# A seventh pair of token blocks, and the operand sums of x moved from the score stage to the expert stage

## The chip, the cores and the metric

The kernel runs on one core of a Trainium2 chip. The metric is device time in microseconds (us), and a shorter time is better. A core has engines that work side by side and wait for each other through semaphores: TensorE (PE in the profile; its weight loads are PEld), VectorE (DVE), ScalarE (ACT), GpSimd (POOL) and SyncE (SP, which here issues nearly all transfers). Each engine works through its own queue in order.

## The reference

The output is x + A(xn) + B(xn), where xn is the layer norm of x (2048 tokens of 512 values, float32).

```python
# A: Fourier mixing, real part
a = einsum("bsd,ed->bse", xn, dft_hid_re);  b = einsum("bsd,ed->bse", xn, dft_hid_im)
A = einsum("ts,bse->bte", dft_seq_re, a) - einsum("ts,bse->bte", dft_seq_im, b)
# B: product-key experts: 32 heads, 64 + 64 keys, 4096 experts, 2 experts per head
q = einsum("nd,dhc->nhc", xn, w_q);  q1, q2 = q[..., :128], q[..., 128:]
s1 = einsum("nhd,ed->nhe", q1, k1);  s2 = einsum("nhd,ed->nhe", q2, k2)
# the 2 best of s1 and of s2 give 4 candidate sums per head; the 2 best of these are the experts
g = softmax(top_s);  ue, ve = u[top_e], v[top_e]
act = gelu(einsum("nd,nhkd->nhk", xn, ue))
B = einsum("nhk,nhk,nhkd->nd", g, act, ve)
```

## The kernel before, in words

The tokens are cut into 16 blocks of 128. Every product of B is made with float16 parts: an operand is split into a high part h and a low part l, and three matmuls (h h, h l, l h) stand for one in float32.

The kernel has three stages. The first, up to about 100 us, makes the layer norm and the Fourier part. The second, the score stage (about 100 to 421 us), makes q and the scores for every block and head group and picks the experts; 128 steps, with a hand-written table `todo` that says which other work is issued at which step: loading and splitting u and v, and sums of operands for the third stage. The third is the expert stage, `part_b` from line 1047 on. It does not gather expert rows. For every block it computes the product with all 4096 rows of u (a "z phase"), applies gelu, multiplies by the gate weights, which are zero for all but the chosen experts, and multiplies the result by all rows of v (a "v phase", `v_part`, 96 matmuls of 128 x 512).

A z phase exists in two forms. A single block (`u_part`, L1095) takes 16 groups of 24 matmuls of 128 x 128: 384. Two blocks together, a pair, can be multiplied with fewer products: for 12 of the 16 groups of u (the three `QUADS`), `z_pair` uses seven products in place of eight for a 2 x 2 block matrix, in Strassen's manner. A product is a `slot` of 24 matmuls (L1168). Some products need a sum of parts of u, which is kept in the DRAM tensor `s_d` and streamed in through a ring of three buffers (`ring_load`), and some need a sum of parts of x, which lies in the tile `x4`. The order of the 21 slots and four plain steps is the string `SEQ`. The slot called 5a, the second of a pair, is the first that reads `x4`. The four remaining groups of u go through `u_part` for both blocks at once (matmuls of 128 x 256). `z_pair` needs VectorE to add products from PSUM (L1204, L1212, L1216) and ScalarE to copy them out and to apply gelu.

The phases before the change are: z(0), z(1), v(0), then for b = 2, 4 .. 12 the pair z(b, b+1), v(b-1), v(b), and at the end z(14), v(13), z(15), v(14), v(15). Thus six pairs and four single blocks.

Between the matmuls of a phase, other work is placed by hand with `put(phase, step, ...)`; a v phase has steps 0 to 7. `G(b, k)` is a one-hot step (`g_mm`): VectorE builds two selection matrices for 16 tokens at a time, L (L1246) and R (L1251, L1254), from the chosen experts, and 32 matmuls (L1256) spread the gate weights over all experts. `W(b, k)` (`w_part`) multiplies them by the gelu values (L1264) and splits the product into two float16 parts (L1271 on ACT, L1272 on VectorE). Four of each are needed for a block before its v phase. The units `U` and `F` are checks: the kernel verifies that the given matrices have the symmetry that its fast Fourier path assumes (`compare`, L1323 on, 68 units `U`) and that the scaled values fit (`fit`, units `F`). They only have to be finished at the end, by `verdict`. `add_x(b)` loads y and x of a block and adds them on POOL (L1314), for all blocks but the last; `finish(b)` (L1318, VectorE) adds the v product, and SP stores it.

The sums of x for a pair are made in the score stage by `sum_x(b, part)` (L817 to L835), at six hand-chosen steps. On POOL: a one-column copy that ties it to its step (L823), one addition of high and low parts, 1024 columns (L824), four subtractions of 256 columns (L829 to L832). Later, on ACT, a rounding to float16 (L794), and on POOL the remainder (L795); then two stores of 256 KB to the DRAM tensor `t_d` (L798). In the expert stage, at the start of v(b), b even, `prep` loads the next two blocks of x into `xb2` (L1077), and SP loads `x4` from `t_d` (L1609). The act tile of a block (`act_tile`) is one of three, used in turn, so that block b+2 takes the one that block b-1 used.

Line by line order on the engines follows the program's order and its data dependencies as the compiler's own scheduler arranges them; some work is moved ahead of its place in the program when its inputs are there.

Of the kernel before, what the change touches and what calls it, by code (L numbers as in the profile page):

```python
# [18 lines left out]
P = 128  # L19
# [10 lines left out]
V1 = 5  # L30
V2 = 9
QUADS = (8, 10, 12, 14), (9, 11, 13, 15), (4, 5, 6, 7)
PAIRS = tuple(range(2, 14, 2))


@with_exitstack
def tile_fnet_peer(ctx, tc, x, ca, cb, c5, wt, wf, wr, wq, kt, ut, vn, out):
# [14 lines left out]
    z_d = dram.tile([NT, P, 3 * P], F16, name="z_d")  # L52
    v_d = dram.tile([16 - V2, P, 4 * D], F16, name="v_d")
    s_d = dram.tile([len(QUADS), 4, P, 4 * D], F16, name="s_d")
    t_d = dram.tile([NT // 2, P, 4 * D], F16, name="t_d")

    stQ = ExitStack()
    PS = [stQ.enter_context(tc.tile_pool(name="psum", bufs=1, space=bass.MemoryType.PSUM))]
# [662 lines left out]
    def part_b(safe, stS, stP, stQ, stE, xt, u_sb, cmp_p, w4):  # L721
# [65 lines left out]
        def scratch(g):  # L787
            return v_sb[g].rearrange("p l c d -> p (l c d)").bitcast(F32)

        def split4(part, t, h, dst, at):  # L790

            l = t.bitcast(F16)[:, 0:2 * D]
            if part == 0:
                nc.scalar.activation(h, t, AF.Copy, scale=behind(one, at))  # L794
                nc.gpsimd.tensor_tensor(l, t, h, op=ALU.subtract)  # L795
                return
            for i, v in enumerate((h, l)):
                nc.sync.dma_start(dst(i), v)  # L798
# [15 lines left out]
            split4(part - 1, s4, v_sb[6].rearrange("p l c d -> p (l c d)")[:, par * 2 * D:par * 2 * D + 2 * D],  # L814
                   lambda i: s_d[qd].rearrange("o p (t l f) -> t l p o f", t=4, l=2)[t, i], at)

        def sum_x(b, part, at=None):  # L817

            n = (0, 2, 4, 4, 7, 5)[PAIRS.index(b)]
            f, t4 = scratch(n), scratch(n + 1)  # L820
            if part == 0:
                v = xq[b // 2]
                nc.gpsimd.tensor_copy(f[:, 0:1], behind(one, at))  # L823
                nc.gpsimd.tensor_tensor(f.rearrange("p (q f) -> p q f", q=2),  # L824
                                        v[:, :, 0].rearrange("p q k n -> p q (k n)"),
                                        v[:, :, 1].rearrange("p q k n -> p q (k n)"), op=ALU.add)
                b11, b21, b12, b22 = [f[:, k * 256:k * 256 + 256] for k in range(4)]
                r = [t4[:, k * 256:k * 256 + 256] for k in range(4)]
                nc.gpsimd.tensor_tensor(r[0], b12, b11, op=ALU.subtract)  # L829
                nc.gpsimd.tensor_tensor(r[1], b22, r[0], op=ALU.subtract)  # L830
                nc.gpsimd.tensor_tensor(r[2], b22, b12, op=ALU.subtract)
                nc.gpsimd.tensor_tensor(r[3], b21, r[1], op=ALU.subtract)  # L832
                return
            split4(part - 1, t4, f.bitcast(F16)[:, 0:2 * D],
                   lambda i: t_d[b // 2, :, i * 2 * D:i * 2 * D + 2 * D], at)  # L835

        SRAW = {}

        def stage_v(g, at, store):
# [159 lines left out]
        if not safe:  # L999
            for n, b in zip((19, 22, 25, 106, 109, 118), PAIRS):  # L1000
                todo[n].append(lambda at, b=b: sum_x(b, 0, at))
                todo[n + (4 if n == 118 else 5)].append(lambda at, b=b: (sum_x(b, 1, at), sum_x(b, 2)))
        for g, n in zip(range(V2, 16), (25, 38, 41, 57, 73, 89, 105)):
            todo[n].append(lambda at, g=g: stage_v(g, at, False))
            todo[n - 3].append(lambda at, g=g: fill_load(1, g))
# [98 lines left out]
        if not safe:  # L1104
            sx = stE.enter_context(tc.tile_pool(name="sx", bufs=1, side="left"))
            x4 = sx.tile([P, 2, 4, 2, P], F16, name="x4")
            PLAIN = [g for g in range(16) if not any(g in q for q in QUADS)]
            SEQ = "1a 5a 2a 6a c 3a 1b 7a 2b 5b 4a 6b c 3b 1c 7b 2c 5c 4b 6c c 3c 7c c 4c".split()

            def turn_q(k, n):  # L1110
                return ("abc" if n % 2 else "cba").index(k)

            OPS = {"1": (0, None, None, 0), "2": (1, None, None, 1), "5": (None, 0, 0, None), "6": (None, 1, 1, None),
                   "3": (None, 3, None, 3), "7": (None, 2, 2, None), "4": (3, None, 3, None)}

        USES = []
        if not safe:
# [393 lines left out]


        phases = [("z", 0), ("z", 1), ("v", 0)]
        for b in range(2, 14, 2):
            phases += [("z", b, b + 1), ("v", b - 1), ("v", b)]
        phases += [("z", 14), ("v", 13), ("z", 15), ("v", 14), ("v", 15)]
        plan = {}

        def put(ph, cg, *fs):
            plan.setdefault((ph, cg), []).extend(fs)  # L1520

        def G(b, k):
            return lambda: g_mm(b, k)
# [16 lines left out]
        for b in range(NT):  # L1540
            ph = ("v", b)
            if b % 2 == 0 and 0 < b < 13:
                nx = phases[phases.index(ph) + 1]
                st = 1 if len(nx) == 2 else 2
                put(ph, 1, G(b + 1, 0))
                put(ph, 3, G(b + 1, 1))
                put(ph, 5, W(b + 1, 0))
                put(ph, 7, W(b + 1, 1), G(b + 1, 2))
                put(nx, st, W(b + 1, 2, True), G(b + 1, 3))
                put(nx, 3 * st, W(b + 1, 3, True))  # L1550
            elif b + 1 < NT:
                for k in range(4):
                    put(ph, 2 * k, W(b + 1, k))
                put(ph, 0, G(b + 1, 2))
                put(ph, 3, G(b + 1, 3))
        for ph in phases[2:]:
            if ph[0] == "z":
                n = 4 * len(ph[1:]) - 2
                put(ph, 5 if len(ph) == 2 else 9, G(ph[1], 0))
                put(ph, 7 if len(ph) == 2 else 12, G(ph[1], 1))  # L1560
        for b in range(14):
            put(("v", b), 3, lambda b=b: compact_d(b + 2))
        if not safe:
            for cg in (1, 3, 5, 7):
                put(("v", 0), cg, F[0])
            for ph, cg in ((("v", 12), 0), (("v", 13), 3), (("v", 14), 3), (("v", 14), 7)):
                put(ph, cg, F[0])
            for ph in phases[3:]:
                if ph[0] == "z":
                    for cg in (8,) if len(ph) == 3 else (1, 3, 4, 5):  # L1570
# [12 lines left out]
            for f, n in ((U, 68), (F[0], NK + 16 - V2), (F[1], 16 + V2)):  # L1583
                assert sum(v.count(f) for v in plan.values()) >= n
        for n, ph in enumerate(phases):
            if ph[0] == "z":
                b = ph[1:]
                for c in b:
                    ACT[c] = BT[c] if c < 2 else act_tile(c)
# [183 lines left out]
```

## Time and profile before

| what | value |
|---|---|
| median of 3 runs | 1130.89 us (1129.87 to 1134.87) |
| the profiled execution | 1132.17 us, span 1130.4 us |
| TensorE clock granted | 0.998 |
| busy: PE, DVE, ACT, POOL | 1114.2, 960.3, 657.5, 319.4 us |
| score stage, 100 to 421 us: busy PE, DVE, POOL | 319.3, 292.2, 258.5 us |
| expert stage, 465 to 1103 us: busy PE, DVE, POOL | 634.3, 532.7, 24.8 us |

The span is the time from the first to the last instruction in the trace; the profiled execution's own time is somewhat longer. Busy time is the time in which an engine had an instruction running; an instruction that is held up after it has begun also counts as busy. A row of a group names the line, the engine, the operation, what is written and read, the number of instructions, then the busy time, the mean of one in ns and the idle time of the engine before them. A row of the timeline names the start, the length and the same, and in brackets how long the engine had been idle before and what ended that.

### The profile page before, as it was taken

What the parts mean: (1) busy time and instruction counts of PE and PEld (TensorE: products, weight loads), DVE (VectorE), ACT (ScalarE), POOL (GpSimd) and SP (SyncE); (2) the same over time, 40 slices, a digit from 0 to 9 for tenths busy, and PEclk for the clock granted to TensorE, in tenths of its full rate; (3) what the DMA queues carried; (4) which work ended last, traced back from release to release, by engine and by line L of the source; (5) the groups of instructions that cost most, each with busy time, mean ns of one, the idle gap of its engine ahead of it and who ended that gap; (6) DMA issues with size and microseconds to landing.
All of it is one profiled execution on the core that took longest, in us unless ns stands there. A gap on an engine that the chain in (4) does not pass through costs nothing.

```text
span 1130.4 us, 28284 instructions
## 1 busy us (share of the span) xinstructions
PE 1114.2 (99%) x11180; PEld 724.4 (64%) x11180; DVE 960.3 (85%) x2873; ACT 657.5 (58%) x1099; POOL 319.4 (28%) x357
## 2 busy tenths in 40 slices
PE   9999999999999999999999999999999999999997
PEld 6455454544545459788588479479569569567763
DVE  7899979989889899976996896896998887889782
ACT  6557598798898465454446446445435535545552
POOL 1416896888889750000000000000010010000000
PEclk9999999999999999999999999999999999999999
DMA  9984455345353315464755755665656756575742
GB/s 274 289 207 171 162 168 197 112 154 190 105 187 103 104 50 190 157 249 143 258 216 184 239 206 199 235 218 187 226 199 215 227 199 225 190 246 167 239 150 106
DMA packets 122540, 213.10 MB, mean 189 GB/s; under 512 B 34580, under 2 KB 62107, under 8 KB 122398
## 3 DMA queue, kind: packets, MB, share of 16 engines
q1 hardware_dynamic: 122096, 211.13, 56.3%
q8 instruction: 89, 1.46, 0.5%
q14 instruction: 53, 0.43, 0.1%
q10 hardware_dynamic: 302, 0.08, 0.1%
HBM read 178.34 MB, written 27.07 MB: 182 GB/s over the span
## 4 chain that ended last, share of the span: by engine, by line
PE 50%; DVE 10%; DMA 3%; ACT 2%; POOL 2%; issue 1%; SPq 0%; DVEq 0%; ACTq 0%; POOLq 0%
PE v L1301 24%; PE z L1168 13%; PE z L1095 10%; PE g L1256 4%; DMA cx<-in_cb_dram 3%; DVE L L1246 2%; DVE vals L956 1%; DVE idx L960 1%; DVE w L1264 1%; DVE act L1272 1%; DVE cx L1351 1%; DVE R L1251 0%; DMA fit<-in_wq_dram 0%; DVE cx L1340 0%; POOL v L824 0%
## 5 line engine op out<-in xcount | busy, mean ns | idle before, releaser
L252 PE MATMUL s<-m,xq 128*128 128x512 f16 x1344 | 297.4, 379 | 1.0 <-ACT ss L952 0.5
L1301 PE MATMUL v<-v,act 128*128 128x512 f16 x1056 | 233.4, 379 | 1.0 <-DMA v<-v_d 1.0
L252 PEld LDWEIGHTS <-xq 128*128 128x128 f16 x1344 | 129.8, 98 | 152.2 <-issue 2.4
L1314 POOL TENSOR_TENSOR y<-y,xr 128x512 f32<-128x512 f32 x15 | 26.1, 1740 | 623.4 <-DMA y<-y_d 383.7
L1246 DVE TENSOR_TENSOR L<-io_lam,cmp 128x2048 f16<-128x2048 f16 x128 | 157.5, 1230 | 26.9 <-PE g L1256 26.8
L1301 PEld LDWEIGHTS <-act 128*128 128x128 f16 x1056 | 101.2, 98 | 118.7 <-issue 1.3
L1095 PE MATMUL z<-xb,u 128*128 128x128 f16 (+1 forms) x2112 | 154.3, 234 | 0.1
L1095 PEld LDWEIGHTS <-u 128*128 128x128 f16 x2112 | 141.4, 98 | 6.6 <-issue 0.2
L956 DVE MAX8 vals<-ss 128x8 f32<-128x64 f32 x896 | 133.5, 216 | 5.6 <-ACT ss L952 5.6
L1301 PE MATMUL v<-v,w 128*128 128x512 f16 x480 | 106.3, 379 | 0.1
L952 ACT ACTIVATE ss<-s,wsc 128x512 f32<-128x512 f32 x120 | 81.4, 682 | 41.2 <-PE s L252 35.1
L1377 ACT ACTIVATE cx<-cx 128x896 f32<-128x896 f32 x64 | 60.4, 944 | 72.6 <-DVE cx L1357 53.2
L1168 PEld LDWEIGHTS <-s 128*128 128x128 f16 x1656 | 94.8, 98 | 0.1
L960 DVE FIND_INDEX8 idx<-vals,ss 128x8 uint16<-128x256 f32 x224 | 93.8, 419 | 0.0
L1271 ACT ACTIVATE act<-w 128x1024 f16<-128x1024 f32 x36 | 48.3, 1357 | 68.3 <-DVE w L1264 68.0
L1301 PEld LDWEIGHTS <-w 128*128 128x128 f16 x480 | 45.9, 98 | 53.6 <-issue 0.4
L1168 PE MATMUL z<-x,s 128*128 128x128 f16 x1248 | 78.1, 219 | 0.0
L1168 PEld LDWEIGHTS <-u 128*128 128x128 f16 x1296 | 74.9, 98 | 1.8 <-issue 1.4
L1256 PEld LDWEIGHTS <-L 128*128 128x128 f16 x2048 | 60.3, 96 | 12.7 <-issue 2.1
L1351 DVE TENSOR_TENSOR cx<-cx 128x512 f32<-128x512 f32 (+2 forms) x84 | 48.4, 613 | 23.5 <-DMA cx<-in_cb_dram 23.5
L1264 DVE SCALAR_TENSOR_TENSOR w<-act,scl,g 128x1024 f32<-128x1024 f32 x44 | 55.8, 1277 | 10.3 <-ACT act L1195 10.3
L1256 PE MATMUL g<-R,L 128*128 128x32 f16 x2048 | 61.9, 176 | 1.6 <-DVE R L1254 1.5
(363 smaller groups left out, 1802.3 us busy)
## 6 DMA issues: line engine op xcount, KB each, us to landing
v<-v_d SPq DMA_DIRECT2D x67, 512.0 KB, 4.3
s<-s_d SPq DMA_DIRECT2D x59, 512.0 KB, 4.8
cx<-in_cb_dram SPq DMA_DIRECT2D x64, 448.0 KB, 4.7
w<-in_wq_dram SPq DMA_DIRECT2D x28, 512.0 KB, 6.0
fit<-in_wq_dram SPq DMA_DIRECT2D x28, 512.0 KB, 4.3
uv<-in_vn_dram SPq DMA_DIRECT2D x16, 512.0 KB, 3.5
uv<-in_ut_dram SPq DMA_DIRECT2D x16, 512.0 KB, 4.2
s_d<-v SPq DMA_DIRECT2D x24, 256.0 KB, 3.7
```

Source lines behind the costliest of these rows:

```text
L252: nc.tensor.matmul(ps, xt[i][:, l, kd, :], m[:, r, kd, :], start=(n == 0), stop=(n == 3 * KD - 1))
L952: nc.scalar.activation(s, ps, AF.Copy, scale=inv)
L956: nc.vector.max(vals[:, i, w, :, h], s[:, g, :])
L960: nc.vector.max_index(idx[:, i, w].rearrange("p k h -> p (k h)"), vals[:, i, w, 0:2].rearrange("p k h -> p (k h)"), s[:, w * HC:g + 1, :]. ...
L1095: nc.tensor.matmul(ps if n == 1 else ps.rearrange("p (b n) -> p b n", b=2), ug[:, l, c % 2, kd, :], xb2[:, k0, r, kd, :] if n == 1 else xb ...
L1168: nc.tensor.matmul(bank[:, t * P:(t + 1) * P], lt, rt, start=(t == k == 0 and op in "125"), stop=(t == 3 and k == 5), skip_group_check=op ...
L1246: nc.vector.tensor_tensor(L.rearrange("p t (l two) -> p t l two", two=2), io_lam.rearrange("p (l two) -> p l two", two=2).unsqueeze(1).to_ ...
L1256: nc.tensor.matmul(p[:, hf, t * NC:(t + 1) * NC], L[:, t, :], R[:, t, :], start=True, stop=True)
L1264: nc.vector.scalar_tensor_tensor(w, act[:, :, ts], fw, p.rearrange("p h (n c) -> p c (h n)", c=NC), op0=ALU.mult, op1=ALU.mult)
L1301: nc.tensor.matmul(pv, w16[:, c, :, l], v_sb[g][:, r, cc, :], start=(n + cc == 0 and k == 0), stop=(n == 15 and cc == 1 and k == 2))
L1351: nc.vector.tensor_tensor(v, v, tv[:, 0:1].to_broadcast([P, len(ix), 256]), op=o)
L1377: later.append(lambda: nc.scalar.activation(tf[:, P:], tf[:, P:], AF.Abs, accum_out=chk[:, n:n + 1]))
```

## The change

The blocks 14 and 15 become a seventh pair: the phases end with z(14, 15), v(13), v(14), v(15). The table `PAIRS` gets the entry 14. `t_d`, `sum_x` and its places in the score stage's table are removed. A new function, `x_sums`, makes the sums of x in the expert stage, at the start of v(b), b even, right after `prep` has issued the loads of the next two blocks: on POOL the addition and four subtractions, from `xb2`, with the not yet used act tile of block b+2 as scratch; at step 5 of the same phase ACT rounds them into `x4`, and POOL writes the remainder into `x4`. The load of `x4` goes. The checks are spread anew: four in each pair phase in place of three, one in v(13) in place of three, three in v(14) as before; the one-hot steps of block 15 go to v(13).

```diff
-PAIRS = tuple(range(2, 14, 2))
+PAIRS = tuple(range(2, NT, 2))
...
-    t_d = dram.tile([NT // 2, P, 4 * D], F16, name="t_d")
...
-        def sum_x(b, part, at=None):
...
-            for n, b in zip((19, 22, 25, 106, 109, 118), PAIRS):
-                todo[n].append(lambda at, b=b: sum_x(b, 0, at))
-                todo[n + (4 if n == 118 else 5)].append(lambda at, b=b: (sum_x(b, 1, at), sum_x(b, 2)))
...
+        def x_sums(b, part):
+
+            s = ACT[b].rearrange("p c n -> p (c n)")
+            f, t4 = s[:, 0:2 * D], s[:, 2 * D:4 * D]
+            if part == 0:
+                nc.gpsimd.tensor_tensor(f.rearrange("p (q f) -> p q f", q=2),
+                                        xb2[:, :, 0].rearrange("p q k n -> p q (k n)"),
+                                        xb2[:, :, 1].rearrange("p q k n -> p q (k n)"), op=ALU.add)
+                b11, b21, b12, b22 = [f[:, k * 256:k * 256 + 256] for k in range(4)]
+                r = [t4[:, k * 256:k * 256 + 256] for k in range(4)]
+                nc.gpsimd.tensor_tensor(r[0], b12, b11, op=ALU.subtract)
+                nc.gpsimd.tensor_tensor(r[1], b22, r[0], op=ALU.subtract)
+                nc.gpsimd.tensor_tensor(r[2], b22, b12, op=ALU.subtract)
+                nc.gpsimd.tensor_tensor(r[3], b21, r[1], op=ALU.subtract)
+                return
+            h, l = [x4[:, n].rearrange("p o k n -> p (o k n)") for n in range(2)]
+            nc.scalar.activation(h, t4, AF.Copy)
+            nc.gpsimd.tensor_tensor(l, t4, h, op=ALU.subtract)
...
-        for b in range(2, 14, 2):
+        for b in range(2, NT, 2):
             phases += [("z", b, b + 1), ("v", b - 1), ("v", b)]
-        phases += [("z", 14), ("v", 13), ("z", 15), ("v", 14), ("v", 15)]
+        phases += [("v", 15)]
...
+        put(("v", 13), 5, G(15, 0))
+        put(("v", 13), 7, G(15, 1))
...
-        for b in range(14):
+        for b in range(13):
             put(("v", b), 3, lambda b=b: compact_d(b + 2))
+        put(("z", 14, 15), 8, lambda: compact_d(15))
...
-                    for cg in (9, 12, 15) if len(ph) == 3 else (0, 2, 3, 6):
+                    for cg in (9, 11, 13, 15):
                         put(ph, cg, U)
                 elif ph[1] < 14:
                     for cg, f in enumerate((None, F[1], F[1], None, U, U, U, F[0]) if ph[1] % 2 == 0 else (
-                            None, F[1], None, None, U, U, U, F[0])):
-                        if f:
+                            None, F[1], F[0], None, U, U, U, F[0])):
+                        if f and (ph[1] < 13 or f != U or cg == 6):
                             put(ph, cg, f)
...
-                if phases[n + 1][1] in PAIRS and not safe:
-                    nc.sync.dma_start(x4.rearrange("p l o k n -> p (l o k n)"), t_d[phases[n + 1][1] // 2])
+                c = phases[n + 1][1]
+                if c in PAIRS and not safe:
+                    ACT[c] = act_tile(c)
+                    x_sums(c, 0)
+                    put(ph, 5, lambda c=c: x_sums(c, 1))
```

More of the change, by code (lines that the diff above doesn't have):

```diff
@@ L815, in sum_u @@
                    lambda i: s_d[qd].rearrange("o p (t l f) -> t l p o f", t=4, l=2)[t, i], at)
-        def sum_x(b, part, at=None):
[L819 to L835, printed above, removed]
         SRAW = {}
@@ L998, in part_b @@
                 todo[n + 5].append(lambda at, g=g: (sum_u(g, 1, at), sum_u(g, 2)))
-        if not safe:
-            for n, b in zip((19, 22, 25, 106, 109, 118), PAIRS):
-                todo[n].append(lambda at, b=b: sum_x(b, 0, at))
-                todo[n + (4 if n == 118 else 5)].append(lambda at, b=b: (sum_x(b, 1, at), sum_x(b, 2)))
         for g, n in zip(range(V2, 16), (25, 38, 41, 57, 73, 89, 105)):
@@ L1555, in part_b @@
                 put(ph, 3, G(b + 1, 3))
+        put(("v", 13), 5, G(15, 0))
+        put(("v", 13), 7, G(15, 1))
         for ph in phases[2:]:
             if ph[0] == "z":
-                n = 4 * len(ph[1:]) - 2
-                put(ph, 5 if len(ph) == 2 else 9, G(ph[1], 0))
-                put(ph, 7 if len(ph) == 2 else 12, G(ph[1], 1))
-        for b in range(14):
+                put(ph, 9, G(ph[1], 0))
+                put(ph, 12, G(ph[1], 1))
+        for b in range(13):
             put(("v", b), 3, lambda b=b: compact_d(b + 2))
+        put(("z", 14, 15), 8, lambda: compact_d(15))
         if not safe:
@@ L1565, in part_b @@
                 put(("v", 0), cg, F[0])
-            for ph, cg in ((("v", 12), 0), (("v", 13), 3), (("v", 14), 3), (("v", 14), 7)):
+            for ph, cg in ((("v", 12), 0), (("v", 14), 1), (("v", 14), 3), (("v", 14), 7)):
                 put(ph, cg, F[0])
@@ L1569, in part_b @@
                 if ph[0] == "z":
-                    for cg in (8,) if len(ph) == 3 else (1, 3, 4, 5):
+                    for cg in (8,):
                         put(ph, cg, F[0])
-                    for cg in (9, 12, 15) if len(ph) == 3 else (0, 2, 3, 6):
+                    for cg in (9, 11, 13, 15):
                         put(ph, cg, U)
@@ L1588, in part_b @@
                 for c in b:
-                    ACT[c] = BT[c] if c < 2 else act_tile(c)
+                    if c not in ACT:
+                        ACT[c] = BT[c] if c < 2 else act_tile(c)
                 def after(cg):
```

## The prediction

> **What bounds the kernel now.** First the page's head, to see which engine is full; then the waits of TensorE in the expert stage alone, from 421 us to the end, because a busy share over the whole span says nothing of one stage. (A wait's columns: us in total, times, longest.)
>
> ```profile
> span 1130.4 us, 28284 instructions
> PE 1114.2 (99%) x11180; PEld 724.4 (64%) x11180; DVE 960.3 (85%) x2873; ACT 657.5 (58%) x1099; POOL 319.4 (28%) x357
> ```
>
> ```profile
> PE g L1256 <- DVE R L1254: 1.5, 3, 1.0
> ...
> PE z L1168 <- ACT act L1215: 0.2, 1, 0.2
> ```
>
> TensorE is busy 99% of the span, and in 710 us of expert stage its five rows of waits make 3.4 us. So matmul time that goes counts in full, and what only relieves another engine counts for nothing, unless TensorE waits for that engine next. How near the others are is read from windows by stage: the scores, v(0), v(6), the last pair z(12,13), and v(13), z(15), v(14). (Columns: window, its length, then busy us of PE, PEld, DVE, ACT, POOL, and the granted clock.)
>
> ```profile
> 100.00:421.00 321.00, 319.33 (x2050) 159.65 (x2048) 292.18 (x1536) 253.74 (x422) 258.53 (x291) 1.00 0.42 136
> 465.00:488.00 23.00, 22.70 (x188) 11.14 (x184) 23.00 (x30) 10.66 (x14) 0.00 (x0) 1.00 0.66 231
> 725.00:748.00 23.00, 23.00 (x187) 11.56 (x185) 18.70 (x30) 7.45 (x12) 1.28 (x1) 1.00 0.59 203
> 923.00:964.00 41.00, 41.00 (x707) 39.93 (x704) 31.74 (x52) 21.84 (x40) 2.36 (x1) 1.00 0.54 191
> 1034.00:1057.00 23.00, 22.70 (x191) 11.31 (x188) 22.97 (x37) 10.04 (x13) 0.00 (x0) 1.00 0.54 192
> 1057.00:1080.00 23.00, 23.00 (x427) 22.65 (x426) 14.62 (x37) 14.47 (x27) 1.28 (x1) 1.00 0.54 172
> 1080.00:1103.00 23.00, 23.00 (x193) 11.65 (x189) 20.27 (x40) 12.29 (x16) 0.00 (x0) 1.00 0.60 184
> ```
>
> VectorE is the second bound, close behind: all of v(0), 18.7 of 23 us in v(6), 31.7 of 41 in a pair. The clock is 1.00 throughout.
>
> **What TensorE saves.** Stretches of the chain of waits (start, length, matmuls) in the last pair, in the single block z(15) and at the end, and the group of the pair's additions:
>
> ```profile
> 928.71 2.62 PE z L1095 x24
> 931.33 0.79 PE g L1256 x32
> 932.12 9.39 PE z L1168 x168
> ...
> 1057.77 16.08 PE z L1095 x288
> ...
> 1099.94 23.97 PE v L1301 x111
> ```
>
> ```profile
> L1204 DVE TENSOR_TENSOR act<-z,act 128x512 f32<-128x512 f32 x9 | 6.2, 686 | 0.0
> ```
>
> A single block takes 384 matmuls at 16.08/288 = 55.8 ns, so z(14) and z(15) cost 768 x 55.8 ns = 42.9 us. As a pair they are 21 slots of 24 matmuls at 9.39/168 = 55.9 ns (28.2 us) and four plain steps of 2.62 us (10.5 us): 38.7 us. The one-hot steps (L1256) and the v phases stay the same in number. Saved: 4.2 us. The pair adds nine VectorE additions of 0.69 us, 6.2 us in a stretch that, by z(12,13), keeps 9 us free: nothing on the path.
>
> **What leaves the scores.** Six times, on POOL, a one-column copy, an addition, four subtractions and a rounding; on ACT two one-column copies and a rounding; on SP two stores; and later, on SP, a load of x4:
>
> ```profile
> L795 POOL TENSOR_TENSOR v<-v,v 128x1024 f16<-128x1024 f32 x18 | 38.4, 2133 | 5.5 <-ACT v L794 5.5
> L824 POOL TENSOR_TENSOR v<-xq 128x1024 f32<-128x1024 f16 x6 | 12.7, 2121 | 0.4
> L831 POOL TENSOR_TENSOR v<-v 128x256 f32<-128x256 f32 x6 | 4.4, 737 | 0.0
> ```
>
> ```profile
> x<-t_d SPq DMA_DIRECT2D x6, 512.0 KB
> s<-s_d SPq DMA_DIRECT2D x59, 512.0 KB, 4.8
> xb<-xt_d SPq DMA_DIRECT2D x14, 256.0 KB, 3.0
> ```
>
> One pair's POOL work is 2.12 + 4 x 0.73 + 2.13 = 7.2 us. In the scores TensorE is busy 319.3 of 321 us, so 43 us less of POOL there are worth 0 to the 1.7 us that TensorE idles. I take 0: it is hidden by TensorE's own work now, and so is its removal. Of DMAs, 6 loads and 12 stores go and about ten loads of s_d come (59 serve six pairs); the DMA engines are at 0.5 to 0.7 in the windows, so 0. On SP the load of x4 stood right behind the loads of xb; what is behind it starts one issue earlier, 0.
>
> **What comes into v(b), b even.** Seven times the same 7.2 us of POOL, in v(0), v(2) to v(12), and a rounding on ACT, which has 12 us and more free there: 0. The first POOL operation waits for xb2's load (3.0 us) and for v(b-1) to free its act tile, so the five start with v(b). Behind them in POOL's queue stands only the addition of y and x for v(b), which VectorE's last step of v(b) needs some 20 us later: 0. x4 is due at the pair's second slot, 24 us after the start, against 7.2 us and ACT's rounding. So POOL is not late. But it does not run beside VectorE for free. Rows of POOL and VectorE around three y additions (start, length):
>
> ```profile
> 560.55 1.22 DVE L1246 TENSOR_TENSOR L<-io_lam,cmp 128x2048 f16<-128x2048 f16 x1
> 560.63 2.26 POOL L1314 TENSOR_TENSOR y<-y,xr 128x512 f32<-128x512 f32 x1 [61.76 <-DVE R L1254]
> 561.71 2.38 DVE L1272 TENSOR_TENSOR act<-w,act 128x1024 f16<-128x1024 f32 x1
> ...
> 996.72 1.39 POOL L1314 TENSOR_TENSOR y<-y,xr 128x512 f32<-128x512 f32 x1 [66.24 <-DVE w L1264]
> 996.89 2.30 DVE L1246 TENSOR_TENSOR L<-io_lam,cmp 128x2048 f16<-128x2048 f16 x1
> 999.12 1.28 DVE L1272 TENSOR_TENSOR act<-w,act 128x1024 f16<-128x1024 f32 x1
> ...
> 1018.30 2.12 POOL L1314 TENSOR_TENSOR y<-y,xr 128x512 f32<-128x512 f32 x1 [20.18 <-DMA y<-y_d]
> 1019.19 1.29 DVE L1264 SCALAR_TENSOR_TENSOR w<-act,scl,g 128x1024 f32<-128x1024 f32 x1
> ```
>
> At 996.9 an L took 2.30 us, not 1.22, because a POOL addition of 1.39 had begun. At 560.6 POOL began while an L ran and took 2.26 us itself, and then VectorE's L1272 took 2.38, not 1.28. They run one after the other, and VectorE loses some 1.1 us to a POOL operation of 1.4. Where VectorE takes an operand from PSUM (the w at 1019.2) it loses nothing.
>
> The Trainium skill (SBUF — State Buffer, "Who interferes with whom") says that a DVE instruction with two SBUF inputs contends with a GpSimd instruction that reads SBUF, and that one with at most one SBUF input, outside the 2-port modes, does not. The trace agrees: 2.30 against 1.22 us, and 1.29 us unharmed. If every VectorE operation stood in the way, the rule would charge 7.2 us at each of seven places, and the sum would be +46 us and not the one below.
>
> What VectorE's loss costs TensorE differs by phase. In v(0), where VectorE never rests (rows of VectorE and TensorE; in brackets the idle time before a row):
>
> ```profile
> 464.59 1.23 DVE L1246 TENSOR_TENSOR L<-io_lam,cmp 128x2048 f16<-128x2048 f16 x1 [1.52 <-PE g L1256]
> 471.44 0.43 DVE L1254 TENSOR_TENSOR R<-R,cmp 128x512 f16<-128x512 f16 x1
> 471.93 0.56 PE L1256 MATMUL g<-R,L 128*128 128x32 f16 x16 [0.19 <-DVE R L1254]
> 489.95 0.43 DVE L1338 TENSOR_TENSOR cx<-cx 128x256 f32<-128x256 f32 x1 [0.56 <-DMA cx<-in_cb_dram]
> ```
>
> VectorE works without a pause from 464.6 to 489.4, and the one-hot matmul at 471.93 starts 0.06 us after its R ends. What VectorE loses ahead of the last one-hot step of v(0), TensorE loses too. The second xb load can only start when z(1) ends at 465, so the sums begin near 468: 2.1 + 4 x 0.73 = 5.0 us in turn with VectorE, and perhaps part of the last 2.1. Bounds 0 (all of it behind the last one-hot step) and 7.2; I take 5.
>
> In the other six there is slack. In v(6), which starts at 725.0:
>
> ```profile
> 730.82 1.23 DVE L1246 TENSOR_TENSOR L<-io_lam,cmp 128x2048 f16<-128x2048 f16 x1 [2.51 <-PE g L1256]
> 745.67 0.46 DVE L1254 TENSOR_TENSOR R<-R,cmp 128x512 f16<-128x512 f16 x1
> 747.37 0.95 PE L1256 MATMUL g<-R,L 128*128 128x32 f16 x32
> ```
>
> VectorE idles 2.5 us before 730.8, and half of the five operations fall there or beside PSUM operations. What is left of them and the rounding of 2.1 us make it some 2.3 us late (between 0 and 5). The one-hot step at 747.37 needs the R that ends at 746.13: 1.2 us of slack. So TensorE waits about 1.1 us. Bounds 0 and 5.0 - 1.2 = 3.8 a phase; I take 1, as v(6) gives, six times: 6.
>
> **The tail.** Until now z(15) lay between v(13) and v(14), and VectorE rested there (14.6 of 23 us). Now v(13) follows the pair and v(14) follows v(13), and the two one-hot steps of z(15), about half of its 14.6 us, go to v(13), from which two checks are taken out. VectorE then has 23.0 + 20.3 + 7.3 less up to 4, some 47 to 50 us, against 2 x 96 matmuls of 23.97/111 us and six steps of 0.79, 46.2 us of TensorE. The checks can go on in v(15), so VectorE need not hold TensorE up; with checks ahead of the last w part it does, by up to 3.8. Bounds -1.5 (the waits for R that there are now go) and 3.8; I take 0.5, near the first, since checks are not waited for.
>
> **Sum.** -4.2 + 5 + 6 + 0.5 = +7.3 us. The profiled execution took 1132.17 us, 1.8 more than its span, and lies 1.3 above the median of 1130.89. On the median: 1130.9 + 7.3 = 1138.2 us.
>
> **Rivals.** (1) TensorE-bound, not slower. POOL's sums land in VectorE's idle time and beside its PSUM operations, and only the 4.2 us show: 1126.7 us; if the old 3.4 us of waits go too, 1123.3. For it: the y additions on POOL cost TensorE no more than 1.5 us in all now. Against it: they are one operation a phase, the sums are six. It decides below 4.2/7 = 0.6 us of wait a pair.
>
> (2) Half of it. v(0) pays and the others absorb, or the reverse: -4.2 + 5 or -4.2 + 6, some 1132 us.
>
> (3) x4 late. ACT's rounding is put at step 5 of 8, some 15 us into v(b), and POOL's last 2.1 to 4 us follow, which leaves about 4 us.
>
> ```profile
> ACT act L1271 <- DVE w L1264: 68.0, 28, 4.6
> ```
>
> A rounding queued behind such a wait, 4.6 us at the longest, makes slot two late by 1 to 2 us: 7 to 14 us on top of -4.2, or of the sum, 1134 to 1152 us.
>
> (4) The last blocks do not run as a pair. The diff leaves no path for it, so it gets no chance of its own.
>
> **How the numbers follow.** 0.5% is 5.7 us, about what a measurement of this kernel can tell from no change. My sum, ending above +5.7: 0.48, its own range 1136.6 to 1149 (with 3 us a phase in place of 1). x4 late or a tail that piles up: 0.07. Half: 0.17. TensorE-bound: 0.28, of which 0.15 stays within 0.5% and 0.13, with old waits gone, passes it. So slower 0.55, same 0.32, faster 0.13. The range must take in most of rival 1: from 1126 to 1149, which leaves out about 0.1 at each end.
>
> **What would show it.** L1168 with 3528 matmuls, not 3024, L1095 with 1440, not 2112, and the last pair in 38.7 us beside its one-hot steps. In v(0), v(2) to v(12), six POOL rows from the phase's start, some far above 0.73 us, and VectorE's L, R and L1272 beside them at twice their time. TensorE's wait for R at 8 to 14 us, not 1.5, some 5 of it in v(0). I am wrong if that wait stays under 4 us, or if TensorE waits for ACT or x4 instead.

## The result and the profile after

The changed kernel took 1150.01 us (median of six, 1147.43 to 1152.92), the kernel before, run beside it, 1132.54 us (six, 1129.87 to 1135.82). The ratio is 1.0155 with a 95% interval of 1.0129 to 1.0181: 17.5 us slower, where 1138.2 us and at most 1149 were predicted. The profiled execution took 1147.43 us, the fastest of the six. (Of the experiments below, one execution of the kernel with fewer checks ran slow, 1434.06 us at a granted clock of 0.75, and its ratio leaves that one out.)

First the head of the page, then the waits of TensorE in the expert stage (us in total, times, longest), and of the kernel before the rows that the prediction did not print:

```profile
span 1145.6 us, 27970 instructions
PE 1112.3 (97%) x11012; PEld 720.4 (63%) x11012; DVE 987.2 (86%) x2882; ACT 664.5 (58%) x1104; POOL 341.5 (30%) x357
```

```profile
PE g L1250 <- DVE R L1248: 15.1, 11, 2.9
PE v L1295 <- DMA v<-v_d: 4.1, 5, 1.7
PE z L1162 <- ACT act L1209: 2.8, 3, 1.9
PE z L1162 <- ACT w L1209: 0.2, 1, 0.2
```

```profile
PE v L1301 <- DMA v<-v_d: 1.0, 1, 1.0
PE z L1168 <- ACT w L1215: 0.4, 1, 0.4
PE z L1168 <- ACT act L1102: 0.3, 1, 0.3
```

L1250 is the one-hot step (L1256 before), L1295 the v matmuls (L1301), L1162 the pair's slots (L1168). TensorE has 1.9 us less of work than before and 17.1 us more of idle time (1145.6 - 1112.3 = 33.3 against 1130.4 - 1114.2 = 16.2). The four rows make 22.2 us, against 3.4. The largest is the one that the prediction named, but over a quarter of the new waiting (5.2 of 18.8 us) is for two things that it had at nothing: loads of v_d and ScalarE.

The start of v(0), rows of VectorE, GpSimd and TensorE (start, length; idle time before in brackets):

```profile
465.39 2.11 DVE L1248 TENSOR_TENSOR R<-R,cmp 128x512 f16<-128x512 f16 x1
467.42 1.74 DVE L1240 TENSOR_TENSOR L<-io_lam,cmp 128x2048 f16<-128x2048 f16 x1
469.09 1.82 DVE L1266 TENSOR_TENSOR act<-w,act 128x1024 f16<-128x1024 f32 x1
473.67 2.35 DVE L1245 TENSOR_TENSOR R<-io_c,cmp 128x512 f16<-128x512 f16 x1
```

```profile
465.09 2.12 POOL L1096 TENSOR_TENSOR w<-xb 128x1024 f32<-128x1024 f16 x1 [17.12 <-issue]
468.05 1.71 POOL L1103 TENSOR_TENSOR w<-w 128x256 f32<-128x256 f32 x1
469.71 1.76 POOL L1102 TENSOR_TENSOR w<-w 128x256 f32<-128x256 f32 x1
473.50 2.24 POOL L1108 TENSOR_TENSOR x<-w,x 128x1024 f16<-128x1024 f32 x1 [1.17 <-ACT x L1107]
```

```profile
467.55 0.55 PE L1250 MATMUL g<-R,L 128*128 128x32 f16 x16 [1.69 <-DVE R L1248]
473.81 0.56 PE L1250 MATMUL g<-R,L 128*128 128x32 f16 x16 [2.24 <-DVE R L1248]
477.60 0.55 PE L1250 MATMUL g<-R,L 128*128 128x32 f16 x16 [1.71 <-DVE R L1248]
481.79 0.56 PE L1250 MATMUL g<-R,L 128*128 128x32 f16 x16 [0.17 <-DVE R L1248]
```

An R of 0.42 us takes 2.11 beside GpSimd's addition and 2.35 beside its remainder; subtractions of 0.73 take 1.71 and 1.76. TensorE waits 5.8 us in these four rows. Of the rest of the R row, 3.8 us lie in v(8), 2.9 in v(12), 1.2 in v(14), 0.9 in v(2) and 0.5 in z(1).

The clock is the second surprise. TensorE around the end of v(8) and in v(12), and 2 us windows of TensorE over the same places (the window, its length, busy us, then granted clock, DMA share, GB/s):

```profile
849.16 0.59 PE L1250 MATMUL g<-R,L 128*128 128x32 f16 x16 [2.37 <-DVE R L1248]
849.58 2.55 PE L1162 MATMUL z<-xb,u 128*128 128x128 f16 x24
851.97 1.50 PE L1162 MATMUL z<-x,s 128*128 128x128 f16 x24
...
1015.84 0.59 PE L1250 MATMUL g<-R,L 128*128 128x32 f16 x16 [2.89 <-DVE R L1248]
```

```profile
848.00:850.00 2.00, 0.84 (x21) 0.60 0.00 0
850.00:852.00 2.00, 2.00 (x23) 0.55 0.30 113
...
1016.00:1018.00 2.00, 2.00 (x21) 0.50 0.91 369
```

Around the ends of the waits of 2.37 and 2.89 us the clock falls to half for some 3.5 us: 24 matmuls take 2.55 us and not 1.50. The fall begins while TensorE still waits, and that part costs nothing. From the end of each wait on, (1 - clock) x time is 1.3 us at the first place (0.65 over 3.84 us) and 1.6 at the second (0.61 over 4.16 us), 2.9 us on top of the waits. A wait of 2.24 us in v(0), between other waits, had no such effect.

### The profile page after: what moved, and what is told of

It reads as the page before. It is cut to its first block, busy times and chain, and to the rows that moved or that the text cites. A ratio compares the mean times of both kernels' runs of the same rounds, so it can differ in the third digit from the quotient of the medians.

```text
span 1145.6 us, 27970 instructions
## 1 busy us (share of the span) xinstructions
PE 1112.3 (97%) x11012; PEld 720.4 (63%) x11012; DVE 987.2 (86%) x2882; ACT 664.5 (58%) x1104; POOL 341.5 (30%) x357
## 4 chain that ended last, share of the span: by engine, by line
PE 63%; DVE 19%; DMA 9%; ACT 3%; issue 3%; POOL 1%; SPq 1%; DVEq 0%; ACTq 0%; POOLq 0%
PE s L251 26%; PE z L1162 14%; PE v L1295 11%; PE z L1070 8%; DVE L L1240 3%; DVE act L1266 3%; PE g L1250 3%; DMA cx<-in_cb_dram 2%; DVE w L1258 2%; DMA v<-v_d 2%; PE m L147 1%; DVE R L1248 1%; DMA fit<-in_wq_dram 1%; DVE R L1245 1%; DVE cx L1334 1%
## 5 line engine op out<-in xcount | busy, mean ns | idle before, releaser
L1295 PE MATMUL v<-v,act 128*128 128x512 f16 x1056 | 235.1, 380 | 2.3 <-DMA v<-v_d 2.3
L1295 PEld LDWEIGHTS <-act 128*128 128x128 f16 x1056 | 101.6, 98 | 121.4 <-issue 5.0
L1070 PE MATMUL z<-xb,u 128*128 128x128 f16 (+1 forms) x1440 | 121.6, 244 | 0.0
L1070 PEld LDWEIGHTS <-u 128*128 128x128 f16 x1440 | 107.6, 98 | 7.2
L1162 PEld LDWEIGHTS <-s 128*128 128x128 f16 x1944 | 111.3, 98 | 0.2
L1295 PE MATMUL v<-v,w 128*128 128x512 f16 x480 | 106.5, 379 | 1.7 <-DMA v<-v_d 1.7
L1162 PE MATMUL z<-x,s 128*128 128x128 f16 x1464 | 91.7, 219 | 0.0
L1162 PEld LDWEIGHTS <-u 128*128 128x128 f16 x1512 | 88.4, 99 | 3.9 <-issue 3.5
L1295 PEld LDWEIGHTS <-w 128*128 128x128 f16 x480 | 45.9, 98 | 55.4 <-issue 2.3
L1096 POOL TENSOR_TENSOR act<-xb 128x1024 f32<-128x1024 f16 x4 | 13.0, 3248 | 221.6 <-PE v L1295 165.4
L1250 PEld LDWEIGHTS <-L 128*128 128x128 f16 x2048 | 60.8, 96 | 26.9 <-issue 11.3
L1250 PE MATMUL g<-R,L 128*128 128x32 f16 x2048 | 62.4, 176 | 15.1 <-DVE R L1248 15.1
L1345 DVE TENSOR_TENSOR cx<-cx 128x512 f32<-128x512 f32 (+2 forms) x84 | 53.3, 670 | 22.8 <-DMA cx<-in_cb_dram 22.8
```

The source lines that it names most:

```text
L1070: nc.tensor.matmul(ps if n == 1 else ps.rearrange("p (b n) -> p b n", b=2), ug[:, l, c % 2, kd, :], xb2[:, k0, r, kd, :] if n == 1 else xb ...
L1162: nc.tensor.matmul(bank[:, t * P:(t + 1) * P], lt, rt, start=(t == k == 0 and op in "125"), stop=(t == 3 and k == 5), skip_group_check=op ...
L1250: nc.tensor.matmul(p[:, hf, t * NC:(t + 1) * NC], L[:, t, :], R[:, t, :], start=True, stop=True)
L1295: nc.tensor.matmul(pv, w16[:, c, :, l], v_sb[g][:, r, cc, :], start=(n + cc == 0 and k == 0), stop=(n == 15 and cc == 1 and k == 2))
L1345: nc.vector.tensor_tensor(v, v, tv[:, 0:1].to_broadcast([P, len(ix), 256]), op=o)
```

## The experiments

Theory: GpSimd's sums take VectorE's time beside the one-hot steps, and TensorE waits for R. Rival A: the seventh pair and the respread checks cost the time. Rival B: it lies in the transport (x4 no longer loaded, another order on SP).

### The pair alone, the sums alone

The first kernel has the seventh pair and all other edits, but forms the sums in the scores and loads x4, with one sum more:

```
- for n, b in zip((19, 22, 25, 106, 109, 118), PAIRS):
+ for n, b in zip((19, 22, 25, 106, 109, 118, 28), PAIRS):
...
- x_sums(c, 0); put(ph, 5, lambda c=c: x_sums(c, 1))
+ nc.sync.dma_start(x4..., t_d[c // 2])
```

> The seventh pair as in the change, but the sums of x made in the score stage and brought through DRAM as before (a seventh sum at step 28). Theory (POOL's sums in the expert stage hold VectorE, and TensorE then waits for R): without them the pair's 4.2 us show, ratio to before 0.996, about 1128 us; TensorE's wait for R falls from 15.1 us to 3 or less, and no wait stands in v(0). Rival A (the tail without z(15), the checks spread anew, or the new order of the queues make VectorE late): the time stays near that of the change, 1140 us or more, with the waits for R at the phases' ends still there.

The second is the reverse: the kernel before, its six pairs and single blocks, with the sums in the even v(b) by `x_sums`.

```
- for n, b in zip((19, 22, 25, 106, 109, 118), PAIRS):
-     todo[n].append(lambda at, b=b: sum_x(b, 0, at))
...
- nc.sync.dma_start(x4..., t_d[phases[n + 1][1] // 2])
+ x_sums(c, 0); put(ph, 5, lambda c=c: x_sums(c, 1))
```

> Six pairs and four single blocks as before, and only the sums of x moved to the expert stage (six of them). Theory: about 5.6 us in v(0) and 5 to 8 us in the others, some 12 to 20 us slower than before, 1145 to 1152 us, with a wait for R of 10 us or more. Rival A: within 3 us of before.

The pair alone: 1134.79 us, ratio 1.0016 (0.9999 to 1.0033). The sums alone: 1148.74 us, ratio 1.0142 (1.0118 to 1.0166). Waits of TensorE with the sums alone:

```profile
PE g L1271 <- DVE R L1269: 10.3, 10, 2.2
PE v L1316 <- DMA v<-v_d: 4.6, 4, 1.6
PE z L1183 <- ACT w L1230: 2.2, 3, 1.2
PE z L1183 <- ACT act L1230: 1.8, 2, 1.5
```

So the move of the sums makes nearly all of the loss, 16 of 17.5 us, and rival A falls. Waits for v_d and ScalarE come with it too, though ScalarE is waited for with the pair alone as well (4.5 us). But the pair, which should have gained 4 us, gains nothing here; that is taken up below.

### GpSimd or the sums as such; how much a microsecond of GpSimd costs

In one kernel the six operations of `x_sums` run on VectorE itself; in another GpSimd makes the addition and the four subtractions twice.

```
- nc.gpsimd.tensor_tensor(...)      # each of the six in x_sums
+ nc.vector.tensor_tensor(...)
```

> The change with the six POOL operations of x_sums done by VectorE itself. VectorE then pays for its own six operations, about 1.1 + 4 x 0.3 + 1.1 = 3.4 us a pair in place of up to 7.2 us of waiting. Theory: between the change and e1, about 1138 to 1144 us; in v(0) a wait for R of about 3 us and not 5.8. Rival B (any added work in VectorE's queue or in ACT's hurts as much, it is not POOL's hold): no better than the change, 1150 us.

```
+ for _ in range(2):
      nc.gpsimd.tensor_tensor(f, xb2[:, :, 0], xb2[:, :, 1], op=ALU.add)
      nc.gpsimd.tensor_tensor(r[0], b12, b11, op=ALU.subtract)
...
```

> The changed kernel, with the addition and the four subtractions that GpSimd makes at the start of each even v(b) made twice over; results and everything else as they are. Theory (GpSimd's time in these operations is taken from VectorE): 5.0 us more of GpSimd work in each of seven phases, of which v(0) passes on 3 to 5 us and the others, whose slack is used up, 2 to 4 each: TensorE's wait for R from 15.1 to 30 us or more, the time 1165 to 1180 us. Rival (the cost comes from elsewhere in the move: x4 no longer a load, the order of DMAs on SP): GpSimd has time to spare, x4 is still in time, 1147 to 1153 us.

On VectorE: 1140.39 us, ratio 1.0070 (1.0050 to 1.0091). Doubled on GpSimd: 1178.42 us, ratio 1.0395 (1.0359 to 1.0431). Waits in the first, then in the second:

```profile
PE g L1250 <- DVE R L1248: 5.7, 7, 2.4
PE v L1295 <- DMA v<-v_d: 4.5, 5, 1.2
```

```profile
PE g L1251 <- DVE R L1249: 23.1, 14, 4.5
PE v L1296 <- DMA v<-v_d: 15.1, 5, 5.4
```

The same work costs 10 us less when the fuller engine does it: an addition of 128x1024 takes 1.21 us on VectorE, and on GpSimd 2.12 us in v(0) and 4.34 in v(8), in turn with VectorE. As the main cause rival B falls with the doubling, which moves no DMA and costs 28 us. More of that came as waits for v_d (+11.0) than for R (+8.0), and the mean granted clock of the profiled executions went from 0.995 to 0.981: GpSimd's hold is paid in more places the later VectorE gets. Whether the 7.6 us that remain with the sums on VectorE are its own time, the respread checks or something of the transport, these runs do not tell apart.

### Where in the phases: v(0), and the checks

One kernel ties the first pair's sums to the last R of v(0)'s one-hot steps. Another leaves out the 37 checks of the v phases.

```
- x_sums(c, 0); put(ph, 5, lambda c=c: x_sums(c, 1))
+ if c > 2: x_sums(c, 0)
+ else: put(ph, 3, lambda c=c: x_sums(c, 0, LR[-1][1][:, 0, 0:1]))   # part 0 after the last R
+ put(ph, 5, lambda c=c: x_sums(c, 1))
```

> The change with the sums of the first pair tied to the last R of v(0)'s own one-hot steps, so that they start after these. Theory: the 5.6 us of waits for R in v(0) go, the rest stays: about 5 us less than the change, 1145 us. Rival C (the wait in v(0) comes from another order or from late loads): the waits in v(0) stay, 1150 us.

```
- units = iter([... for n in range(68)])
+ units = iter([... for n in range(31)])
- if f and (ph[1] < 13 or f != U or cg == 6):
+ if f and f != U:
```

> The changed kernel with the 37 checks of the v phases left out (two to three comparisons of 2.2 us of VectorE in each of v(1) to v(13), with their loads and ScalarE passes); those of the pairs stay. It leaves out a part of the check that decides whether the fast path holds. Theory (GpSimd's hold costs TensorE only where VectorE has no idle time to take it): v(0), which never had such a check, keeps its 5.8 us of waits for R, and those of v(2) to v(12), 9.3 us, fall under 2; with the slow clock behind the long ones, 1136 to 1140 us. Rival (the sums lie on the way of the one-hot steps wherever they run): waits for R stay above 12 us, 1145 us or more.

The first took 1147.91 us (1.0129, 1.0104 to 1.0153). v(0) is free of waits but for 0.16 us, and z(2,3) has them now, of which these are the two largest:

```profile
490.11 1.44 PE L1164 MATMUL z<-x,s_-1_6737 128*128 128x128 f16 x23 [1.26 <-POOL x L1110]
495.84 2.78 PE L1070 MATMUL z<-xb,u 128*128 128x256 f16 x24 [1.60 <-DVE y L1314]
```

The waits of z(2,3) add to 5.9 us: what v(0) gained came back, since x4 was late and VectorE still behind. The time is not told apart from the change's (1.0155, 1.0129 to 1.0181), where the theory had 5 us less. Without the 37 checks the time is 1131.39 us, ratio 0.9993 (0.9974 to 1.0013), below what any theory had:

```profile
PE g L1250 <- DVE R L1248: 6.2, 5, 2.2
```

v(0), which never held such checks, keeps 5.1 of the 6.2 us; 8.9 us of waits for R go, and the row of v_d with them, 4.1 us, which the expectation had not taken off. So TensorE waits little beside GpSimd's sums where VectorE has room. No run left the same checks out of the kernel before, so what they cost there is not taken off, and the checks' own loads are gone too.

### Why v_d is late

At the end of v(2), SP issued the load of a large check only after waiting 5.8 us for VectorE (0.2 us before the change), and in v(6) the store of the block before after 4.6 us; loads of v_d stand behind both. The row of the first, from the waits of SP's queue between 568 and 582 us:

```profile
SPq L1422 <- DVE sums L1326: 5.8, 1, 5.8
```

Three kernels move these: the large check of an even v(b) into the next pair; the store to the fourth part of the next phase; and both, the store after the seventh part.

```
- (None, F[1], F[1], None, U, U, U, F[0]) if ph[1] % 2 == 0
+ (None, F[1], F[1], None, U, U, U, None) if ph[1] % 2 == 0
- for cg in (8,):
+ for cg in (8,) if ph[1] == 2 else (4, 8):
```

> The changed kernel with the large check at the end of each even v(b) moved to step 4 of the next pair; no work is left out. Theory (SP takes its loads in order: that check's load waits up to 5.8 us for a buffer that VectorE, held up, gives back late, and the load of v_d behind it comes too late): the waits for v_d fall from 4.1 to 1 us or less, the waits for R stay at 13 to 16 us, and the time is 3 to 5 us shorter, 1145 to 1147 us. Rival (v_d is late for another reason, such as the transfers of that stretch): waits for v_d of 3 to 5 us and 1149 to 1151 us.

```
- nc.sync.dma_start(out[b * P:(b + 1) * P], y)
+ STORE.append(lambda: nc.sync.dma_start(out[b * P:(b + 1) * P], y))
...
  v_part(b, pv, cg)
+ if cg == 3: store()
```

> The changed kernel with the store of each finished block to the output issued after the fourth part of the next phase instead of at its start; no work is left out. Theory (SP takes its queue in order; the store of v(b-1) waits there for VectorE's last step on y, which comes late where GpSimd has held VectorE up, 4.6 and 8.8 us in the rows of v(6) and v(2), and the loads of v_d for v(b) stand behind it): the waits for v_d fall from 4.1 to 1 us or less, waits for R stay at 12 to 16, time 1145 to 1147 us. Rival (v_d is late for want of bandwidth in that stretch, whatever the order): v_d stays at 3 to 6 us and the time at 1149 to 1152.

> The changed kernel with both edits at once: the large check of an even v(b) in the next pair, and the store of a finished block after the seventh part of the next phase. Theory (each edit alone left the other load or store in front of the loads of v_d on SP, and the store, moved by four parts only, still waited 4.5 us for VectorE at 737.7 us): with both out of the way the waits for v_d fall to 1.5 us or less; the time 1147 to 1152 us, since the moved check makes z wait for ScalarE 3 us more. Rival (v_d is late because the buffers come free late or the transfers are slow there): v_d stays at 3 to 6 us.

They took 1154.69 us (1.0201, 1.0174 to 1.0227), 1149.68 (1.0165, 1.0146 to 1.0184) and 1157.92 (1.0236, 1.0175 to 1.0297); the rows of v_d, in this order:

```profile
PE v L1295 <- DMA v<-v_d: 5.3, 5, 2.1
```

```profile
PE v L1295 <- DMA v<-v_d: 3.3, 3, 1.8
```

```profile
PE v L1295 <- DMA v<-v_d: 4.7, 3, 2.1
```

The sums of the waits stay, and the moved check adds 4 to 6 us of waits of z for ScalarE, so as an account of the whole row the theory falls. (The second row is of an execution of 1142.42 us, 7 us below that kernel's median.) By place it does better. The wait of 1.10 us in v(2), behind the check's load, is in neither kernel that moves the check; other waits are new or longer there, up to 2.1 us each. And the late store tested little: in v(6) it was issued at 737.67 us, against 737.58 in the change, since it still waited for VectorE. In the kernel before it waits there too, 4.7 us, without a wait for v_d in v(6).

Where the wait is long, the trace names the step. With the sums doubled, in v(2), a wait of SP's queue, the load of v_d behind it, and TensorE:

```profile
SPq L1423 <- DVE sums L1327: 10.1, 1, 10.1
```

```profile
584.33 0.35 SPq L1287 DMA_DIRECT2D v<-v_d  x1
```

```profile
588.72 4.38 PE L1296 MATMUL v<-v,w 128*128 128x512 f16 x12 [4.70 <-DMA v<-v_d]
```

SP held the check's load for 10.1 us until VectorE gave a buffer back, issued v_d right behind it, and TensorE went on 4.4 us later (a load of v_d takes 4.6 us to land, by the median). In v(4) SP held that load 7.4 us; in v(8) and v(10) it held the load of x for the addition of y, 9.6 and 7.6 us, for GpSimd. A load of v_d follows each, at once or one load later, and the four waits of TensorE behind them make 14.4 of the 15.1 us. So lateness reaches the loads through SP's queue, by more than one load. No run removes it there, and for the 4.1 us of the change, apart from v(2), the step stays open: with the sums on VectorE the row is 4.5 us although the waits for R are down to 5.7.

### Where the pair's 4.2 us went

In the kernel with the pair alone, two rows tell of it, from the scores and from the whole span:

```profile
PE m L149 <- POOL w L168: 2.1, 1, 2.1
```

```profile
PE z L1188 <- ACT act L1235: 3.9, 4, 1.8
```

The first is that experiment's own doing: the seventh sum, at step 28, made GpSimd late for the scores. The second is of the pair with its respread checks, since no sums run beside the phases here. ScalarE's pass over the large check waits for its load, and z's evictions (the copies of products out of PSUM) stand behind it. By the program the pass is queued at step 11 now (checks at 9, 11, 13, 15) and at step 12 before (9, 12, 15). The pass in z(8,9), in the kernel before, in the changed kernel and with the pair alone:

```profile
761.51 1.06 ACT L1429 ACTIVATE fit<-fit 128x1024 f32<-128x1024 f32 x1 [0.51 <-DMA fit<-in_wq_dram]
```

```profile
772.64 1.06 ACT L1423 ACTIVATE fit<-fit 128x1024 f32<-128x1024 f32 x1 [2.53 <-DMA fit<-in_wq_dram]
```

```profile
769.53 1.06 ACT L1449 ACTIVATE fit<-fit 128x1024 f32<-128x1024 f32 x1 [2.93 <-issue]
```

That the pass now comes too early after its load, the theory of the first run below, is not what these traces show. On ScalarE the pass has the same place in all three, behind the same eviction (at 760.42, 769.53 and 766.03 us). Its load is issued 8.2 us after the pair starts in the kernel before and with the pair alone, 9.8 in the change. What differs besides is the time from that issue to the pass: 5.1 us before, 6.1 in the change, 7.5 with the pair alone. Why it is longer stays open.

Four kernels take this back step by step, each keeping the edits of the one ahead: the load at step 7; the last three checks in v(15); the seventh sum at step 42; and the late store.

```
- for cg in (8,): put(ph, cg, F[0])
+ for cg in (7,): put(ph, cg, F[0])
```

> The kernel with the seventh pair alone (sums in the scores), with the load of the large check in a pair issued one step earlier (7, not 8). Theory (the respread checks ate the pair's gain: with checks at 9, 11, 13, 15 ScalarE reaches that check's pass three steps after its load was issued, where it was four with 9, 12, 15, and waits for the load with z's evictions behind it): the waits of z for ScalarE fall from 4.5 to about 1 us, and the time from 1134.8 to 1130 or 1131 us. Rival (the pair saves nothing, or the wait comes back elsewhere): 1134 to 1136 us, and other rows of waits.

```
- put(("v", 14), cg + 4, U)
- put(("v", 15), cg, F[1])
+ put(("v", 15), cg, F[1], U)
```

> The kernel with the seventh pair alone, the early load in the pairs, and the last three checks put into v(15) instead of v(14). Theory (VectorE is full in v(13) and v(14), which follow one another now): the two waits for R there, 1.8 us, go too: 1128 to 1130 us, below the kernel before. Rival (the checks hold up the last additions and the verdict at the end of v(15)): 1131 to 1136 us, and waits behind the last v.

```
- zip((19, 22, 25, 106, 109, 118, 28), PAIRS)
+ zip((19, 22, 25, 106, 109, 118, 42), PAIRS)
```

> The kernel with the seventh pair alone, early loads and the last three checks in v(15), with the seventh sum at step 42 of the scores instead of 28. In the two runs before it, TensorE waited 2.1 us for GpSimd at 174 us, in the scores (m for w), a wait that the kernel before does not have. Theory (the pair does save 4.2 us, and that wait gives half of it back): the wait goes, GpSimd being idle for a third of 170 to 190 us, and the time falls by 2 us, to 1129.5 to 1130.5 us. Rival (the pair saves nothing): the wait goes or moves and the time stays at 1131.5 to 1133 us.

> The best kernel so far (the seventh pair alone, its sum at step 42 of the scores, early loads in the pairs, last checks in v(15)) with the same late store. Theory: its 1.5 us of waits for v_d go as well, 1127 us against 1128.3. Rival (no lateness to take away where the sums are not beside the one-hot steps): 1128 to 1129 us.

They took 1133.36 us (ratio 1.0007, 0.9987 to 1.0027), 1132.36 (1.0003, 0.9988 to 1.0019), 1128.31 (0.9973, 0.9959 to 0.9987) and 1129.39 (0.9984, 0.9966 to 1.0001). With the early load z's waits for ScalarE are 1.9 us, not 4.5, but it is not shown that the edit did it: in z(8,9) that load is again issued 8.2 us after the start, and the waits are 1.7 us with the sums on VectorE, where the load is not moved. The gain in time, 0.1% by the ratios, lies within the intervals, and so does that of the tail. The third kernel is 3.1 us below the kernel before (interval 1.5 to 4.6, which holds the 4.2). The late store gains nothing more. The third kernel's largest row of waits, over the whole span:

```profile
PE g L1276 <- DVE R L1274: 2.8, 5, 1.1
```

The 2.1 us in the scores are gone, and no row is above 2.8 us. What the pair saves can be read from the first matmul of v(0) to the end of the span, in the kernel before and in the third:

```profile
465.20 2.54 PE L1301 MATMUL v<-v,act 128*128 128x512 f16 x11
```

```profile
466.99 2.53 PE L1321 MATMUL v<-v,act 128*128 128x512 f16 x11
```

That is 665.2 us of a span of 1130.4, and 664.3 of 1131.3. The third kernel has 3.0 us more of waits in it (6.4 against 3.4), so its matmuls take 3.9 us less; with the late store, in the same way, 4.4. The pair does save TensorE about what was worked out, if nothing beside it is made late. (That third profile's span is above its kernel's median; its clock was 0.80 in the first 25 us, where the profile of the kernel before had 1.00.)

## Why the prediction was wrong

The direction and the main mechanism held, and the size did not. Its terms against the profiled executions, in us, from the first matmul of v(0) to the end of the span. In the changed kernel that matmul is

```profile
463.33 2.54 PE L1295 MATMUL v<-v,act 128*128 128x512 f16 x11
```

| term | predicted | measured |
|---|---|---|
| matmuls of the seventh pair | -4.2 | -3.9, in the third kernel with the pair alone |
| waits for R: v(0), six v(b), tail | +11.5 | +13.1 (14.6 - 1.5) |
| waits for v_d (SP and DMAs at 0) | 0 | +3.1 (4.1 - 1.0) |
| waits of z for ScalarE (ACT at 0) | 0 | +2.1 (3.0 - 0.9) |
| half clock after long waits ("1.00 throughout") | 0 | +2.9 (1.3 + 1.6) |
| sum | +7.3 | +17.3; the stretches differ by 17.1 (682.3 - 665.2) |
| ahead of v(0) ("What leaves the scores": 0) | 0 | -1.9 (463.3 - 465.2) |

So the terms account for the loss in these executions. The 1.9 us ahead of v(0) are no gain that is shown: three other kernels without the sums in the scores reach v(0) at 463.2, 464.8 and 466.9 us.

- **What TensorE saves**: right in size, but "nothing on the path" left out what came with it. The respreading of the checks, in the diff, was given no cost beside the tail; with the pair alone z waits 4.5 us for ScalarE, against 0.9.
- **v(0), +5**: 5.6 more than before (5.8 - 0.2), in the place and by the mechanism named, though the sums began at 465.1 us and not near 468. But TensorE's wait is not what the phase is worth: put off, it came back in z(2,3).
- **The other six, +1 each**: 8.8 us of R waits lie outside v(0) and z(1), 7.5 more than before, where 6.5 were predicted, tail included. The total is near, but by some luck, since they were not even. v(6) had slack enough (none), while v(8) waited 3.8 and v(12) 2.9. The step took v(6), in which VectorE was least busy, as the pattern of all. The upper bound of 3.8 a phase held for the waits; with the half clock behind it v(8) lost more.
- **The rule on GpSimd and VectorE** held. The Trainium skill (SBUF — State Buffer, "Who interferes with whom") has a two-SBUF-input VectorE instruction contend with a GpSimd one that reads SBUF, and "Issue order, not op shape, decides who blocks"; the R of 2.11 beside an addition of 2.12, and the subtractions of 1.71, agree. Its full price of 7.2 us in seven places was not reached: waits for R rose by 13.6 in the whole expert stage.
- **x4 late** did not happen in the change (no wait names it), and did when the sums were put off (1.26 us). **TensorE-bound** fell; without the 37 checks the changed kernel is level with the kernel before (0.9993), still not at the 1126.7 of that rival.
- The step that failed is the list of zeros: SP, DMAs, ACT and the clock, put at nothing, came to 8.1 of the 10 us that the sum missed. They were read from the kernel before, where VectorE is in time: loads issued early, ScalarE with 12 us free, a clock of 1.00. VectorE's lateness took away the first and the last. For ScalarE that is not shown, since the pair alone has that wait without the sums. The sign of being wrong that the prediction gave, TensorE waiting for ACT, came true in part.

## What to carry to other kernels

A second engine that is 95 to 100% busy in some stretches is a bound there. If that engine is VectorE, work for GpSimd beside it is not free: take as the upper bound of its direct wait that it is time of VectorE's own, at the length that it has on GpSimd. When an engine close to the bound is made late, price not only the wait that names it but also what its lateness does to queues behind it (here loads that SP held, with others in line), and ask whether any single wait gets long enough to cost the clock. When small jobs are respread to fill gaps, ask what their loads and passes stand in front of.

## What was not expected of the hardware

A wait of TensorE of 2.4 us was enough to bring its granted clock down, and no length of wait decided it in these traces. Two places, each a one-hot step after its wait and windows of 2 us of TensorE; first with the sums doubled, in v(6), then with both the check and the store moved, in v(12):

```profile
762.61 0.58 PE L1251 MATMUL g<-R,L 128*128 128x32 f16 x16 [1.98 <-DVE R L1249]
```

```profile
762.00:764.00 2.00, 1.39 (x19) 0.68 1.05 257
```

```profile
1031.10 0.55 PE L1250 MATMUL g<-R,L 128*128 128x32 f16 x16 [2.92 <-DVE R L1248]
```

```profile
1032.00:1034.00 2.00, 2.00 (x11) 1.00 0.82 303
```

A wait of 1.98 us halved the clock, and one of 2.92 left it at 1.00. Nor does the price grow with the wait: with the sums doubled, waits of 4.70 and 2.49 us both cost 1.7 us of clock, while behind one of 2.25 us in v(0), in the kernel with the check moved, the half clock lasted twice as long and cost 3.4. The Trainium skill (TensorE: Matmul & The Clock Gate, "Part 1: The HAM clock gate") gives half the clock after an idle window of about 3.4 us, and about as long a busy time to get it back. The half clock and, at most places, the 3.5 us agree with the windows here; the idle time does not, at 2.0 to 2.5 us, and the measurement decides.
